# One ring for all loads, alternating K and V, and a column-tiled PV in a decode block with a 32768-row cache

## The chip, the cores and the metric

The kernel runs on one core of one Trainium2 chip; the other cores are idle. The metric is the device time of the execution in microseconds (us). Executions of one kernel agree within 1% here. Engine names are those of the profile: PE is TensorE (PEld its weight loads), DVE is VectorE, ACT is ScalarE, POOL is GpSimd, SP is SyncE, which in this kernel only issues the loads and the output.

## The reference, cut to what matters

A transformer block for one new token, batch 2, all in bf16. The cache is large, everything else is small:

```python
B, Sq, D = (2, 1, 1024);  Hq, Hkv, Sk, Dh = (32, 4, 32768, 128);  F = 3584
mod = silu(c) @ w_mod                       # [1024, 6144], gives sa, ca, ga, sb, cb, gb
h = layernorm(x) * (1 + ca) + sa
q = h @ wq                                  # 8 query heads for each of 4 KV heads
o = softmax(q k^T / sqrt(128)) v            # K and V: 2 x 4 x 32768 x 128 each
x = x + ga * (o @ wo)
h = layernorm(x) * (1 + cb) + sb
x = x + gb * (gelu(layernorm(h) @ w1 + b1) @ w2 + b2)   # the MLP has a layer norm of its own
```

K and V are 134.2 MB of the 178.3 MB that have to be read, each byte once. A (batch, KV head) pair is called a group below; there are 8, each with four chunks of K and four of V, 8192 rows or 2 MB to a chunk.

## The kernel before: the parts that matter

A small tracker writes the waits. It keeps, for every named region of memory, a token of its last writer and tokens of its readers since; an operation waits for the tokens of all regions that it names, and then leaves its own token on them.

```python
def _dep_tokens(self, E, reads, writes):
    ...                                    # last writer of each read region
    for w in self._expand(writes):         # last writer and readers of each written one
        reg = self._region(w)
        if reg[0] is not None:
            tokens.append(reg[0])
        tokens.extend(reg[1])
    ...
def _record(self, token, reads, writes):
    for w in writes:                       # the operation becomes last writer of ALL it names
        reg = self._region(w)
        reg[0] = token
        reg[1] = []
    ...
```

Loads go through six slots of 16 KB per partition, used in turn, plus fixed places for WO and W1. Each slot is one region, so two loads meet only when they use the same slot. SP issues the loads in the order of a list; a load waits until the slot's old content has been read.

```python
R = 6
slots = [at(f"slot{i}", [128, SLOT_BYTES // 2], BF16, slot_off(i)) for i in range(R)]
seq += kv("K", 0) + kv("K", 1) + kv("V", 0)            # four K chunks, four V chunks, ...
...
T.dma("sp", lambda e, dst=dst, src=src: e.dma_start(dst, src), key=key, writes=list(it.regions))
```

A whole group's K is transposed and multiplied (`QK(i)`), then the V of the group before (`PV(i-1)`). PV holds a 128 x 128 block of V stationary and streams 8 columns, 64 matmuls a chunk:

```python
T.inst("pe", lambda e, ...: e.matmul(psO[:, 0:HPG], lhsT=sl_view[:, t * 128:(t + 1) * 128],
                                     rhs=E_sb[j][:, :, tg], ...))
```

WO and W2 are loaded as `"(t p) n -> p t n"`, in rows of 2 KB. The layer norm inside the MLP is left out.

Of the kernel before, what the change touches and what calls it, by code (L numbers as in the profile page):

```python
# [12 lines left out]
HQ = 32  # L13
# [6 lines left out]
CH_ROWS = 8192  # L20
TPC = CH_ROWS // 128
NCH = S // CH_ROWS
# [6 lines left out]
R = 6  # L29
NKT = 8  # L30
PIPE = 3
NPKT = 4
NPS = 1
EVAC_PATTERN = ("dve", "act", "dve", "act", "dve", "dve", "act", "dve")
SLOT_BYTES = 16 * 1024
# [161 lines left out]
def bass_adaLN_cond__gqa_block_cached__mixer_channel_mlp__decode_kernel(  # L197
# [17 lines left out]
    ident = nc.alloc_sbuf_tensor("ident", [128, 128], BF16)  # L215
    identf = nc.alloc_sbuf_tensor("identf", [128, 128], FP32)
    onesf = nc.alloc_sbuf_tensor("onesf", [128, 128], FP32)
    x16 = nc.alloc_sbuf_tensor("x16", [16, 128], BF16)
    c16 = nc.alloc_sbuf_tensor("c16", [16, 128], BF16)
    b1m = nc.alloc_sbuf_tensor("b1m", [FT, 128], BF16)  # L220
    b2m = nc.alloc_sbuf_tensor("b2m", [KT8, 128], BF16)
    smallT = nc.alloc_sbuf_tensor("smallT", [128, 68], FP32)
    xT = smallT[:, 0:16].rearrange("p (b k) -> p b k", b=2)
    cT = smallT[:, 16:32].rearrange("p (b k) -> p b k", b=2)
    b1T = smallT[:, 32:60]
    b2T = smallT[:, 60:68]
    sgT = nc.alloc_sbuf_tensor("sgT", [128, 2, KT8], FP32)
    siluT = nc.alloc_sbuf_tensor("siluT", [128, 2, KT8], BF16)
    stat = nc.alloc_sbuf_tensor("stat", [128, 8], FP32)
    mean = nc.alloc_sbuf_tensor("mean", [128, 2], FP32)  # L230
    rstd = nc.alloc_sbuf_tensor("rstd", [128, 2], FP32)
    xc = nc.alloc_sbuf_tensor("xc", [128, 2, KT8], FP32)
    sq = nc.alloc_sbuf_tensor("sq", [128, 2, KT8], FP32)
    t1 = nc.alloc_sbuf_tensor("t1", [128, 2, KT8], FP32)
    hT = nc.alloc_sbuf_tensor("hT", [128, 2, KT8], BF16)
    modT = nc.alloc_sbuf_tensor("modT", [128, NMOD, 2], FP32)
    qacc = nc.alloc_sbuf_tensor("qacc", [128, 2 * HQ], FP32)
    qT = nc.alloc_sbuf_tensor("qT", [128, 2, HQ], BF16)
    attnT = nc.alloc_sbuf_tensor("attnT", [128, 2, HQ], BF16)
    yT = nc.alloc_sbuf_tensor("yT", [128, 2, KT8], FP32)  # L240
    x1T = nc.alloc_sbuf_tensor("x1T", [128, 2, KT8], FP32)
    h2T = nc.alloc_sbuf_tensor("h2T", [128, 2, KT8], BF16)
    zT = nc.alloc_sbuf_tensor("zT", [128, FT, 2], FP32)
    z2 = nc.alloc_sbuf_tensor("z2", [128, FT, 2], FP32)
    z3 = nc.alloc_sbuf_tensor("z3", [128, FT, 2], FP32)
    th = nc.alloc_sbuf_tensor("th", [128, FT, 2], FP32)
    gT = nc.alloc_sbuf_tensor("gT", [128, FT, 2], BF16)
    mT = nc.alloc_sbuf_tensor("mT", [128, KT8, 2], FP32)
    resT = nc.alloc_sbuf_tensor("resT", [128, 2, KT8], FP32)
    res_bf = nc.alloc_sbuf_tensor("res_bf", [128, 16], BF16)  # L250
    res16 = nc.alloc_sbuf_tensor("res16", [16, 128], BF16)
    m1 = [nc.alloc_sbuf_tensor(f"m1_{i}", [128, HPG], FP32) for i in range(2)]
    gm = [nc.alloc_sbuf_tensor(f"gm_{i}", [HPG, 1], FP32) for i in range(2)]
    diag = [nc.alloc_sbuf_tensor(f"diag_{i}", [HPG, HPG], FP32) for i in range(2)]
    negm = [nc.alloc_sbuf_tensor(f"negm_{i}", [128, HPG], FP32) for i in range(2)]
    rowsum = [nc.alloc_sbuf_tensor(f"rowsum_{i}", [128, HPG], FP32) for i in range(2)]
    rinv = [nc.alloc_sbuf_tensor(f"rinv_{i}", [128, HPG], FP32) for i in range(2)]

    KB = 1024
    ARENA = R * SLOT_BYTES + 32 * KB + 32 * KB + 32 * KB  # L260
    arena = nc.alloc_sbuf_tensor("arena", [128, ARENA], mybir.dt.uint8)
    abase = nc.lookup_mloc(arena).addr

    def at(name, shape, dtype, off):
        return nc.alloc_sbuf_tensor_at(name, list(shape), dtype, offset=abase + off)

    def slot_off(sl):
        return sl * SLOT_BYTES

    slots = [at(f"slot{i}", [128, SLOT_BYTES // 2], BF16, slot_off(i)) for i in range(R)]  # L270
    regA = R * SLOT_BYTES
    regB = regA + 32 * KB
    regC = regB + 32 * KB
    wo_blk = [at("wo0", [128, 16, DM], BF16, regA), at("wo1", [128, 16, DM], BF16, regB)]
    w1p = [at(f"w1p{k}", [128, F], BF16, (regA + k * 7 * KB) if k < 4 else (regB + (k - 4) * 7 * KB)) for k in range(6)]
    for i in range(2):
        for q in range(4):
            T.interval(f"wo{i}q{q}", (regA if i == 0 else regB) + q * 8 * KB, (regA if i == 0 else regB) + (q + 1) * 8 * KB)
    for k in range(6):
        off = (regA + k * 7 * KB) if k < 4 else (regB + (k - 4) * 7 * KB)  # L280
        T.interval(f"w1p{k}", off, off + 7 * KB)
    S_sb = at("S_sb", [128, HPG, NCH * TPC], FP32, regC)
    E_sb = [at(f"E_sb{i}", [128, HPG, NCH * TPC], BF16, regC + 8 * KB + i * 4 * KB) for i in range(2)]
    KT_sb = [at(f"KT_sb{i}", [128, 8, 128], BF16, regC + 16 * KB + i * 2 * KB) for i in range(NKT)]
    assert 16 + 2 * NKT <= 32

    psKT = [nc.alloc_psum_tensor(f"psKT{i}", [128, 1024], BF16) for i in range(NPKT)]
    psS = [nc.alloc_psum_tensor(f"psS{i}", [128, 512], FP32) for i in range(NPS)]
    psO = nc.alloc_psum_tensor("psO", [128, 512], FP32)
    psM = nc.alloc_psum_tensor("psM", [128, 512], FP32)  # L290
    psX = nc.alloc_psum_tensor("psX", [128, 512], FP32)

    T.inst("pool", lambda e: e.memset(ident[:, :], 0.0), writes=["ident"])
    T.inst("pool", lambda e: e.affine_select(out=ident[:, :], in_=ident[:, :], compare_op=ALU.not_equal, fill=1.0,
                                             base=0, pattern=[[-1, 128]], channel_multiplier=1), reads=["ident"], writes=["ident"])
    T.inst("pool", lambda e: e.memset(identf[:, :], 0.0), writes=["identf"])
    T.inst("pool", lambda e: e.affine_select(out=identf[:, :], in_=identf[:, :], compare_op=ALU.not_equal, fill=1.0,
                                             base=0, pattern=[[-1, 128]], channel_multiplier=1), reads=["identf"], writes=["identf"])
    T.inst("pool", lambda e: e.memset(onesf[:, :], 1.0), writes=["onesf"])

    T.dma("act", lambda e: e.dma_start(x16[:, :], A_x.rearrange("b o (k p) -> (b o k) p", p=128)), key="ld", writes=["x16"])
    T.dma("act", lambda e: e.dma_start(c16[:, :], c.rearrange("b (k p) -> (b k) p", p=128)), key="ld", writes=["c16"])
    T.dma("act", lambda e: e.dma_start(b1m[:, :], B_b1.rearrange("(f p) -> f p", p=128)), key="ld", writes=["b1m"])
    T.dma("act", lambda e: e.dma_start(b2m[:, :], B_b2.rearrange("(f p) -> f p", p=128)), key="ld", writes=["b2m"])

    class Item:
        def __init__(self, kind, i=0, cc=0, nslots=1, fixed=None):
            self.kind, self.i, self.cc, self.nslots, self.fixed = kind, i, cc, nslots, fixed
            self.pos = None
            self.view = None  # L310
            self.regions = None
            self.issued = False

    def kv(kind, i):
        return [Item(kind, i, cc) for cc in range(NCH)]

    def woq(i, qs):
        return [Item("WO", i, q, fixed="AB") for q in qs]
    K4 = kv("K", 4)
    V3 = kv("V", 3)  # L320
    seq = [Item("WMODH", 0, nslots=2)] + [Item("WQ", k) for k in range(KT8)]
    seq += kv("K", 0) + kv("K", 1) + kv("V", 0)
    seq += [Item("MODB", 0), Item("MODB", 1)] + kv("K", 2) + kv("V", 1)
    seq += [Item("MODB", 2), Item("MODB", 3)] + kv("K", 3) + kv("V", 2)
    seq += [Item("MODB", 4), Item("MODB", 5)] + woq(0, [0, 1]) + K4[0:2] + woq(0, [2, 3]) + K4[2:4]
    seq += [Item("MODB", 6), Item("MODB", 7)] + woq(1, [0, 1]) + V3[0:2] + woq(1, [2, 3]) + V3[2:4]
    seq += kv("K", 5) + kv("V", 4)
    seq += kv("K", 6) + kv("V", 5)
    seq += kv("K", 7) + kv("V", 6)
    seq += [Item("W1", k, fixed="AB") for k in range(4)] + kv("V", 7) + [Item("W1", k, fixed="AB") for k in range(4, 6)]  # L330
    seq += [Item("W1", k) for k in range(6, KT8)] + [Item("W2", j) for j in range(4)]
    lookup = {}
    rpos = 0
    for it in seq:
        lookup[(it.kind, it.i, it.cc)] = it
        if it.fixed is None:
            if it.nslots == 2 and (rpos % R) == R - 1:
                rpos += 1
            it.pos = rpos
            rpos += it.nslots  # L340
            sl = it.pos % R
# [11 lines left out]
            elif it.kind == "W2":  # L353
                it.view = at(f"w2v{it.i}", [128, 7, DM], BF16, slot_off(sl))
# [65 lines left out]
    def need(kind, i, cc=0):  # L420
        it = lookup[(kind, i, cc)]
        if not it.issued:
            issue_until(kind, i, cc)
# [314 lines left out]
```

## Time and profile before

Median 445.67 us of 3 runs (445.67 to 447.52) when the prediction was made.

| what | value | where it is read |
|---|---|---|
| bytes read | 178.28 MB | page, part 3 |
| share of the load queue | 96.7% of 16 engines' span | page, part 3 |
| PE busy | 309.0 of 445.5 us | page, part 1 |
| stream where nothing holds it | 420 to 433 GB/s | page, part 2 |

First the page of the kernel before, parts 1 to 3: busy time, the busy tenths and GB/s of the load engines in 40 slices of 11.1 us, and the queue that carries the loads (packets, MB, share).

```profile
PE 309.0 (69%) x7805; PEld 295.2 (66%) x7805; DVE 157.9 (35%) x294; ACT 143.3 (32%) x251; POOL 1.3 (0%) x9
...
DMA  8999999999999999999999999999999999999990
GB/s 316 421 425 433 419 423 431 420 344 424 425 430 420 427 427 419 414 413 410 417 413 403 428 425 430 422 384 415 430 424 418 427 382 383 427 425 414 394 369 34
...
q1 hardware_dynamic: 21616, 178.27, 96.7%
```

The load engines are busy in nearly every slice: the kernel is bound by the stream, and only the dips (344, 384, 382, 394, 369) and the two ends are to be had. (The 403 to 417 of slices 17 to 22, 178 to 245 us, fall where WO is loaded, in 2 KB rows.) What SP waited for before it could issue a load (SP's own waits; total us, times, longest us):

```profile
SPq L184 <- PE psKT L540: 194.6, 28, 18.0
SPq L184 <- PE psO L595: 77.3, 24, 9.8
...
SPq L184 <- PE psS L468: 13.3, 1, 13.3
```

Nearly every such wait is for PE: mostly the transposes (L540) or PV (L595) still read the slot. While earlier loads are queued, such a wait costs nothing. It costs where the queue runs dry; in stretches of ten microseconds (columns: busy us and number for PE, PEld, DVE, ACT and POOL, granted PE clock, share of the load engines, GB/s):

```profile
90.00:100.00 10.00, 9.39 (x283) 9.02 (x279) 5.15 (x7) 4.03 (x5) 0.00 (x0) 0.98 0.92 339
290.00:300.00 10.00, 8.98 (x228) 8.49 (x224) 5.40 (x9) 5.08 (x6) 0.00 (x0) 1.00 0.96 383
...
420.00:430.00 10.00, 4.95 (x153) 4.74 (x153) 2.57 (x15) 1.49 (x2) 0.00 (x0) 0.50 1.05 387
430.00:440.00 10.00, 6.74 (x247) 6.62 (x244) 2.33 (x12) 0.25 (x1) 0.00 (x0) 0.50 0.50 183
```

The first two are such dry spells. At 420 to 430 us the engines are fully busy (1.05) but move only 387 GB/s: this is W2, in 2 KB rows. At 430 to 440 us the stream ends, and compute alone follows.

### The profile page before, as it was taken

What the parts mean: (1) busy time and instruction counts of PE and PEld (TensorE: products, weight loads), DVE (VectorE), ACT (ScalarE), POOL (GpSimd) and SP (SyncE); (2) the same over time, 40 slices, a digit from 0 to 9 for tenths busy, and PEclk for the clock granted to TensorE, in tenths of its full rate; (3) what the DMA queues carried; (4) which work ended last, traced back from release to release, by engine and by line L of the source; (5) the groups of instructions that cost most, each with busy time, mean ns of one, the idle gap of its engine ahead of it and who ended that gap; (6) DMA issues with size and microseconds to landing.
All of it is one profiled execution on the core that took longest, in us unless ns stands there. A gap on an engine that the chain in (4) does not pass through costs nothing.

```text
span 445.5 us, 16705 instructions
## 1 busy us (share of the span) xinstructions
PE 309.0 (69%) x7805; PEld 295.2 (66%) x7805; DVE 157.9 (35%) x294; ACT 143.3 (32%) x251; POOL 1.3 (0%) x9
## 2 busy tenths in 40 slices
PE   1445987996986698638684258887977698755555
PEld 1445877895986598638574158886976588744455
DVE  1101656551652265215351004551643065400221
ACT  2001556630751166024250004640752065305100
POOL 1000000000000000000000000000000000000000
PEclk9999996995996599657696555995896579855555
DMA  8999999999999999999999999999999999999990
GB/s 316 421 425 433 419 423 431 420 344 424 425 430 420 427 427 419 414 413 410 417 413 403 428 425 430 422 384 415 430 424 418 427 382 383 427 425 414 394 369 34
DMA packets 21807, 179.35 MB, mean 403 GB/s; under 512 B 1770, under 2 KB 1770, under 8 KB 11498
## 3 DMA queue, kind: packets, MB, share of 16 engines
q1 hardware_dynamic: 21616, 178.27, 96.7%
q8 instruction: 61, 1.00, 0.9%
q14 instruction: 8, 0.07, 0.0%
q10 hardware_dynamic: 122, 0.02, 0.0%
HBM read 178.28 MB, written 0.00 MB: 400 GB/s over the span
## 4 chain that ended last, share of the span: by engine, by line
PE 52%; DMA 19%; issue 11%; ACT 9%; SPq 6%; DVE 3%; ACTq 0%; DVEq 0%
PE psKT L540 23%; PE psO L595 10%; DMA slot_53<-in_A_k_cache_dram 10%; PE psS L520 8%; SPq L396 5%; DMA wqv_77<-in_A_wq_dram 5%; DMA slot_54<-in_A_v_cache_dram 4%; PE psM L607 3%; ACT KT_sb_67 L550 3%; ACT S_sb L525 3%; ACT KT_sb_72 L550 2%; ACT E_sb_65 L576 1%; PE psM L572 1%; PE psM L478 1%; PE psM L567 1%
## 5 line engine op out<-in xcount | busy, mean ns | idle before, releaser
L550 ACT ACTIVATE KT_sb_72<-psKT 128x1024 bf16<-128x1024 bf16 x32 | 32.7, 1023 | 44.7 <-PE psKT L540 44.7
L550 ACT ACTIVATE KT_sb_67<-psKT 128x1024 bf16<-128x1024 bf16 x25 | 25.6, 1024 | 58.1 <-PE psKT L540 58.1
L576 ACT ACTIVATE E_sb_64<-S_sb,negm 128x256 bf16<-128x256 f32 x32 | 16.2, 506 | 78.1 <-DVE negm L574 77.3
L540 PE MATMUL psKT<-ident,slot_53 128*128 128x128 bf16 x384 | 35.5, 255 | 8.2 <-DMA slot_53<-in_A_k_cache_dram 8.2
L576 ACT ACTIVATE E_sb_65<-S_sb,negm 128x256 bf16<-128x256 f32 x32 | 16.2, 506 | 61.8 <-DVE negm L574 61.0
L553 DVE COPY KT_sb_70<-psKT 128x1024 bf16<-128x1024 bf16 x32 | 22.1, 692 | 36.2 <-PE psKT L540 36.2
L540 PEld LDWEIGHTS psKT<-ident,slot_53 128*128 128x128 bf16 x384 | 28.7, 116 | 8.4 <-DMA slot_53<-in_A_k_cache_dram 8.3
L540 PE MATMUL psKT<-ident,slot_51 128*128 128x128 bf16 x320 | 28.5, 251 | 4.7 <-DMA slot_51<-in_A_k_cache_dram 4.7
L540 PE MATMUL psKT<-ident,slot_54 128*128 128x128 bf16 x384 | 29.3, 218 | 1.2 <-issue 1.2
L598 DVE TENSOR_TENSOR attnT<-psO,rinv 128x8 bf16<-128x8 f32 x8 | 1.3, 167 | 79.2 <-PE psO L595 79.2
L553 DVE COPY KT_sb_66<-psKT 128x1024 bf16<-128x1024 bf16 x32 | 22.1, 692 | 19.6 <-PE psKT L540 19.4
L553 DVE COPY KT_sb_73<-psKT 128x1024 bf16<-128x1024 bf16 x32 | 22.1, 692 | 19.3 <-PE psKT L540 19.3
L553 DVE COPY KT_sb_68<-psKT 128x1024 bf16<-128x1024 bf16 x32 | 22.1, 692 | 17.9 <-PE psKT L540 17.9
L540 PE MATMUL psKT<-ident,slot_49 128*128 128x128 bf16 x320 | 27.0, 240 | 1.3 <-issue 1.3
L540 PEld LDWEIGHTS psKT<-ident,slot_51 128*128 128x128 bf16 x320 | 23.3, 114 | 5.4 <-DMA slot_51<-in_A_k_cache_dram 4.8
L550 ACT ACTIVATE KT_sb_69<-psKT 128x1024 bf16<-128x1024 bf16 x25 | 25.7, 1028 | 3.3 <-PE psKT L540 3.3
L540 PE MATMUL psKT<-ident,slot_50 128*128 128x128 bf16 x320 | 24.4, 218 | 0.3 <-issue 0.3
L540 PE MATMUL psKT<-ident,slot_52 128*128 128x128 bf16 x320 | 24.3, 218 | 0.0
L540 PEld LDWEIGHTS psKT<-ident,slot_49 128*128 128x128 bf16 x320 | 21.6, 108 | 1.4 <-issue 1.4
L553 DVE COPY KT_sb_71<-psKT 128x1024 bf16<-128x1024 bf16 x32 | 22.1, 691 | 1.0 <-PE psKT L540 0.8
L540 PEld LDWEIGHTS psKT<-ident,slot_54 128*128 128x128 bf16 x384 | 21.8, 97 | 0.0
L525 ACT ACTIVATE S_sb<-psS 128x512 f32<-128x512 f32 x32 | 19.0, 593 | 7.9 <-PE psS L520 7.9
(195 smaller groups left out, 517.1 us busy)
## 6 DMA issues: line engine op xcount, KB each, us to landing
slot_53<-in_A_k_cache_dram SPq DMA_DIRECT2D x6, 2048.0 KB, 15.6
slot_54<-in_A_k_cache_dram SPq DMA_DIRECT2D x6, 2048.0 KB, 17.6
slot_51<-in_A_v_cache_dram SPq DMA_DIRECT2D x6, 2048.0 KB, 17.1
slot_52<-in_A_v_cache_dram SPq DMA_DIRECT2D x6, 2048.0 KB, 19.8
slot_49<-in_A_k_cache_dram SPq DMA_DIRECT2D x5, 2048.0 KB, 17.1
slot_50<-in_A_k_cache_dram SPq DMA_DIRECT2D x5, 2048.0 KB, 20.3
slot_51<-in_A_k_cache_dram SPq DMA_DIRECT2D x5, 2048.0 KB, 19.2
slot_52<-in_A_k_cache_dram SPq DMA_DIRECT2D x5, 2048.0 KB, 19.2
```

The lines of the kernel that those rows point to most:

```text
L396: T.dma("sp", lambda e, dst=dst, src=src: e.dma_start(dst, src), key=key, writes=list(it.regions))
L478: T.inst("pe", lambda e, jc=jc: e.matmul(psM[:, 288 + jc * 2:290 + jc * 2], lhsT=wv[:, jc * 128:(jc + 1) * 128], rhs=siluT[:, :, kb], star ...
L520: T.inst("pe", lambda e, sbk=sbk, sp=sp, kn=kn, jj=jj: e.matmul(psS[sbk][:, sp * HPG:(sp + 1) * HPG], lhsT=KT_sb[kn][:, jj, :], rhs=qT[:, ...
L525: T.inst("act", lambda e, sbk=sbk, col0=col0: e.activation(S_sb[:, :, col0:col0 + 64], psS[sbk][:, 0:512].rearrange("p (t h) -> p h t", h= ...
L540: T.inst("pe", lambda e, kq=kq, jj=jj, sl_view=sl_view, t=t: e.transpose(psKT[kq][:, jj * 128:(jj + 1) * 128], sl_view[:, t * 128:(t + 1) ...
L550: T.inst("act", lambda e, kq=kq, kn=kn: e.activation(KT_sb[kn][:, :, :], psKT[kq][:, 0:1024].rearrange("p (a n) -> p a n", a=8), ACT.Copy) ...
L553: T.inst("dve", lambda e, kq=kq, kn=kn: e.tensor_copy(KT_sb[kn][:, :, :], psKT[kq][:, 0:1024].rearrange("p (a n) -> p a n", a=8)), reads=[ ...
L567: T.inst("pe", lambda e: e.matmul(psM[0:HPG, 0:128], lhsT=m1[j][:, :], rhs=identf[:, :], start=True, stop=True), reads=[f"m1_{j}", "identf ...
L572: T.inst("pe", lambda e: e.matmul(psM[:, 128:128 + HPG], lhsT=onesf[0:HPG, :], rhs=diag[j][:, :], start=True, stop=True), reads=["onesf", ...
L576: T.inst("act", lambda e, h=h: e.activation(E_sb[j][:, h, :], S_sb[:, h, :], ACT.Exp, bias=negm[j][:, h:h + 1], scale=SCALE, accum_out=row ...
L595: T.inst("pe", lambda e, t=t, sl_view=sl_view, tg=tg: e.matmul(psO[:, 0:HPG], lhsT=sl_view[:, t * 128:(t + 1) * 128], rhs=E_sb[j][:, :, tg ...
L607: T.inst("pe", lambda e, wv=wv, t=t, cch=cch: e.matmul(psM[:, col0 + cch:col0 + cch + 1], lhsT=wv[:, t % 16, cch * 128:(cch + 1) * 128], r ...
```

## The change

The intent: keep the stream full from the first byte to the last. All loads go in order through one ring of 160 KB per partition; a K chunk and the V chunk of five steps earlier are used in each step, so that memory comes free evenly; WO and W2 are read in long rows; PV takes a quarter of the matmuls; and the MLP's layer norm, which the reference has, is put in. The core of the diff, cut:

```diff
-R = 6
-SLOT_BYTES = 16 * 1024
+VLAG = 5
+RING = 160 * 1024
...
+    def add(key, shape, src):
+        nbytes = int(np.prod(shape)) * 2
+        off = 0
+        if stream:
+            off = stream[-1].off + stream[-1].nbytes
+            if off + nbytes > RING:
+                off = 0
...
+    for k in range(KT8):
+        add(("wmod", k), [6 * DM], ...)                # 12 KB
+    for k in range(4):
+        add(("wq", k), [2, HQ * D], ...)               # 16 KB
+    for n in range(NK + VLAG):
+        if n < NK: add(("K", n), [TPC, D], ...)        # 16 KB
+        if n - VLAG >= 0: add(("V", n - VLAG), ...)    # 16 KB; a WO quarter, 16 KB, after every eighth V
+    ...                                                # w1: four of 14 KB; w2: 16, 16, 16, 8 KB
+    def need(*key):
+        it = by_key[key]
+        while pos[0] <= it.n:
+            cur = stream[pos[0]]
+            old = [o.reg for o in stream[:cur.n] if o.off < cur.off + cur.nbytes and cur.off < o.off + o.nbytes]
+            T.dma("sp", ..., key=f"d_{cur.reg}", writes=[cur.reg] + old)
+            pos[0] += 1
...
-                e.matmul(psO[:, 0:HPG], lhsT=sl_view[:, t * 128:(t + 1) * 128], rhs=E_sb[j][:, :, tg], ...)
+                e.matmul(psO[32 * q:32 * q + 32, :], lhsT=E_sb[j][:, tg // 4, :, :] (32 columns: 8 heads x 4 rows),
+                         rhs=it.view[:, t4 * 4:t4 * 4 + 4, :] (512 columns), ...)     # q = t4 % 4
...
-  A_wo[r0:r0 + 512, :].rearrange("(t p) n -> p t n", p=128)
+  A_wo[g * 1024:(g + 1) * 1024, :].rearrange("(p j) n -> p j n", j=8)
...
+    layernorm(hmid[:, :, :], ["hmid"])
```

PV now makes four times the products it needs (each of 4 rows against each of 4 V blocks); after a group, a few DVE operations and one matmul pick the diagonal blocks.

## The prediction

> **What bounds the kernel now.** The memory stream. The page counts 178.28 MB read, DMA share 96.7%; in ten-microsecond stretches it moves 420 to 433 GB/s where nothing holds it; PE is busy 309.0 us of 445.5. The Trainium skill ("HBM Reference", Specifications (TRN2)) gives about 425 GB/s for a core that streams alone; this trace agrees. 178.28 MB at 424 GB/s is 420.5 us, so only some 25 us are to be had:
> - start: 306 GB/s in the first 10 us, 2.8 us lost;
> - stalls, where the slot to be refilled is still being read (SP waits for transposes and PV): 339 GB/s at 90-100 us, 383 at 290-300, 378 and 373 at 360-380; about 5.3 us;
> - loads in 2 KB rows (W2: 399 and 387 GB/s at 410-430; WO alike): about 3 us;
> - tail: the stream stops near 434.7 us (183 GB/s at 430-440); GELU, W2 and the output take the last 10.8 us.
>
> **What the change does.**
> 1. Ring: 160 KB of in-order stream against six 16 KB slots plus fixed regions; K and V of a step are used together, so a buffer is free soon after it lands. SP's waits become harmless: minus 5.2 us.
> 2. Rows of WO 16 KB, of W2 8 KB: minus 3 us. Fewer PE instructions to fetch (512 PV matmuls for 2048): minus 0.4.
> 3. Tail: after V's last chunk remain WO, W1, W2: 16.8 MB, 39.5 us of stream. The chain under it: last PV 2, picking the diagonal blocks 5, WO 2, then before's chain from WO to the end (418.4 to 445.5, 27 us) plus 4 for the second layer norm: about 40 us. So W2's last block (32 matmuls, 27 ns each) and before's 3.7 us from the last W2 matmul to the end follow the last byte: 5 us where 10.8 were. Minus 5.5. The second layer norm is hidden.
> 4. PV before: 128 matmuls in 3.57 us, with pauses of 2.6 ("issue"): 2.4 us a chunk. After: 16 matmuls of 512 columns; a transpose of 128 columns takes 60 ns at full clock, so 240 ns each: 3.8 us in series, 1 to 1.6 if the column tiles overlap. The skill ("TensorEngine Tiling (Array Packing)", Theoretical Speedup) allows up to 4x; no run here shows it yet. A K chunk takes PE 5.8 us (distance of score evictions). A K and V pair costs PE 7 to 7.5 us (9.7 in series) against 9.9 of stream (4.19 MB): off the path, barely so in series. ACT and DVE need about 5 us each per pair.
>
> **Sum.** 445.7 - 5.2 - 3.4 - 5.5 = 431; pure stream 420.5 + 2.8 + 5 + 2 for instruction fetch is 430. **Predicted 430 us, 8 in 10 between 424 and 439.** Faster by over 2% (below 436.8): 0.85; within 2%: 0.13; slower: 0.02.
>
> **What the profile would show.** Right: 415 GB/s or more in every slice from the second to the last but one; stream ending about 5 us before the span; PV 1 to 1.6 us a chunk; PE waiting for K or V loads; the last chain through W2's last load. Wrong: slices below 400 in the middle (ring or PE holds the stream); PE never waiting for K (tiles in series); W2 starting well after its last load (layer norms, or W1 with its weights strided by 4 columns, slower than 27 ns each).
>
> **What would make it wrong.** Column tiles in series at a lower PE clock: PE-bound, 440 or more. The exponentials (5.5 us of ACT in one lump) blocking evictions beyond the slack. A tail chain 5 us longer. A different stream rate with K and V alternating.

## The result, and the profile after

534.51 us median of 4 runs (533.38 to 537.57), against 446.43 of before in the same rounds. Ratios here are the mean time of one kernel's runs over that of the other's in the same rounds, so not quite the ratio of the medians; this one is 1.197 (95% interval 1.192 to 1.202). The change made the kernel a fifth slower where 3.5% faster had been forecast.

The page of the changed kernel, the same lines as above (slices of 13.3 us):

```profile
PE 312.0 (59%) x6035; PEld 275.5 (52%) x6035; DVE 164.1 (31%) x344; ACT 160.8 (30%) x266; POOL 1.3 (0%) x9
...
DMA  8999688987779786996889786997869958887665
GB/s 354 428 420 432 270 318 317 430 365 295 318 316 429 312 350 234 424 428 244 345 343 430 313 345 264 362 428 314 321 255 427 424 192 351 333 375 285 263 224 199
...
q1 hardware_dynamic: 14112, 178.27, 83.1%
```

PE's busy time hardly moved, but the stream has holes in the whole middle and tail, with full speed (424 to 432) in between. The engines are idle in the holes (tenths of 5 to 8), so it is not a slower stream but an interrupted one. The prediction had named slices under 400 in the middle as the sign that "ring or PE holds the stream". Which of them, SP's waits tell:

```profile
SPq L339 <- DMA V<-in_A_v_cache_dram: 201.2, 13, 30.2
SPq L339 <- DMA K<-in_A_k_cache_dram: 186.0, 14, 29.8
SPq L339 <- DMA w<-in_B_w_dram: 53.7, 5, 19.5
SPq L185 <- DMA w<-in_B_w_dram: 8.1, 1, 8.1
SPq L339 <- DMA wo<-in_A_wo_dram: 6.9, 1, 6.9
```

This is the line to notice. Before, SP waited for PE. Now it waits 13 + 14 + 5 + 1 + 1 = 34 times for a *load to land* before it issues another load. Loads of K and V write different places and need nothing of each other. The chain of waits in order of time (start us, us, what), one lap of the ring; its short PE and SP pieces are left out:

```profile
88.98 30.69 DMA V<-in_A_v_cache_dram
119.69 7.38 DMA K<-in_A_k_cache_dram
...
127.08 0.33 SPq L339
...
127.46 12.89 DMA K<-in_A_k_cache_dram
...
151.29 30.60 DMA V<-in_A_v_cache_dram
181.92 7.26 DMA wo<-in_A_wo_dram
189.19 0.33 SPq L339
...
189.57 12.10 DMA V<-in_A_v_cache_dram
```

From 119.69 to 127.08 us exactly one load is under way: it was issued when the one before it had landed (88.98 + 30.69), and the next was issued when it had landed itself. Alone it takes 7.38 us, where 2.097 MB at the 429 GB/s of a full slice would take 4.9. No other load is queued, ahead of it or behind it, at that moment.

And PE waits for K, not the other way round. The groups of the changed kernel (columns as in the page's part 5: busy us, mean ns; then the idle time before them and what ended it):

```profile
L541 PE MATMUL psKT<-ident,K 128*128 128x128 bf16 x2048 | 196.5, 254 | 103.7 <-DMA K<-in_A_k_cache_dram 103.7
...
L468 PE MATMUL psO<-V,E_sb 128*32 128x512 bf16 x512 | 40.8, 448 | 27.1 <-DMA V<-in_A_v_cache_dram 27.1
```

### Where the 34 waits come from

They can be derived from the source. `old` lists every item, of any age, whose bytes the new one overlaps. The load names them as `writes`, for a good reason: it has to wait for their readers. But the tracker then makes the load the *last writer of each of them*, dead items included. A dead item under two later ones ties these together. The eight 12 KB modulation items do just that, for good, because they stay in `stream`:

```
ring, KB   0        12   16     24      32  36          48
dead       | wmod0  | wmod1     | wmod2     | wmod3     |
live       | chunk A     | chunk B      | chunk C       |
```

Chunk A overlaps wmod1 and marks it. Chunk B overlaps wmod1 too, finds A's load as its last writer, and waits until A has *landed*. wmod2 ties C to B likewise. At 48 KB both grids meet again (3 x 16 = 4 x 12), so the next chunk is free, and the same pattern follows from 48 to 96 KB; above that lie 16 KB items only. That is four false waits in each lap of ten loads. In the tail the 14 KB items of W1 shift the grid, and each of the eight loads but two (W1's first and third) waits for its predecessor. Going through the 88 loads with these rules gives 34 waits for the load just before: 28 among K, V and WO and 6 among W1 and W2. The profile counted the same: 13 + 14 + 1 and 5 + 1.

### The profile page after: what moved, and what is told of

The parts are those of the page before. It is cut to its first block, busy times and chain, and to the rows that moved or that the text cites. A ratio compares the mean times of both kernels' runs of the same rounds, so it can differ in the third digit from the quotient of the medians.

```text
span 531.6 us, 13037 instructions
## 1 busy us (share of the span) xinstructions
PE 312.0 (59%) x6035; PEld 275.5 (52%) x6035; DVE 164.1 (31%) x344; ACT 160.8 (30%) x266; POOL 1.3 (0%) x9
## 4 chain that ended last, share of the span: by engine, by line
DMA 86%; PE 7%; SPq 6%; issue 1%; DVE 0%
DMA K<-in_A_k_cache_dram 37%; DMA V<-in_A_v_cache_dram 35%; DMA w<-in_B_w_dram 13%; SPq L339 6%; PE psKT L541 5%; DMA wo<-in_A_wo_dram 1%; PE psS L436 1%; DVE KT_sb L547 0%; PE psM L489 0%; PE psM L478 0%; PE psS L586 0%; PE psO L468 0%; PE psM L454 0%; PE psM L448 0%; PE psM L592 0%
## 5 line engine op out<-in xcount | busy, mean ns | idle before, releaser
L541 PE MATMUL psKT<-ident,K 128*128 128x128 bf16 x2048 | 196.5, 254 | 103.7 <-DMA K<-in_A_k_cache_dram 103.7
L541 PEld LDWEIGHTS psKT<-ident,K 128*128 128x128 bf16 x2048 | 150.9, 115 | 119.8 <-DMA K<-in_A_k_cache_dram 116.6
L545 ACT ACTIVATE KT_sb<-psKT 128x1024 bf16<-128x1024 bf16 x96 | 98.3, 1024 | 260.0 <-PE psKT L541 250.4
L547 DVE COPY KT_sb<-psKT 128x1024 bf16<-128x1024 bf16 x160 | 109.1, 690 | 210.6 <-PE psKT L541 209.7
L436 PE MATMUL psS<-qT,KT_sb 128*128 128x8 bf16 x2048 | 93.1, 169 | 4.5 <-ACT KT_sb L545 4.5
L436 PEld LDWEIGHTS psS<-qT,KT_sb 128*128 128x128 bf16 x2048 | 88.0, 103 | 5.5 <-ACT KT_sb L545 4.7
L468 PE MATMUL psO<-V,E_sb 128*32 128x512 bf16 x512 | 40.8, 448 | 27.1 <-DMA V<-in_A_v_cache_dram 27.1
L457 ACT ACTIVATE E_sb<-S_sb,negm 128x256 bf16<-128x256 f32 x64 | 32.5, 508 | 7.5 <-DVE negm L455 5.6
L442 DVE TENSOR_REDUCE m1c<-S_sb 128x8 f32<-128x512 f32 x32 | 22.0, 688 | 14.3 <-ACT S_sb L441 12.7
L457 ACT ACTIVATION_READ_ACCUMULATOR E_sb<-S_sb,negm 128x1 f32 x64 | 12.0, 187 | 0.0
```

What stands on the lines that cost most here:

```text
L436: pe(lambda e, t=t, jj=jj: e.matmul(ps[:, t * HPG:(t + 1) * HPG], lhsT=KT_sb[kn][:, jj, :], rhs=qT[:, b, g * HPG:(g + 1) * HPG], start=Tru ...
L442: dve(lambda e: e.tensor_reduce(m1c[:, :, cc], Sc, AX.X, ALU.max), reads=[f"S_sb{i % 2}_{cc}"], writes=[f"m1c{cc}"])
L457: act(lambda e, h=h: e.activation(E_sb[j][:, :, h, :], S_sb[j][:, h, :].rearrange("p (u t) -> p u t", t=4), ACT.Exp, bias=negm[j][:, h:h + ...
L468: pe(lambda e, t4=t4, tg=tg, q=q: e.matmul(psO[32 * q:32 * q + 32, :], lhsT=E_sb[j][:, tg // 4, :, :].rearrange("p h t -> p (h t)"), rhs=i ...
L541: pe(lambda e, kq=kq, jj=jj, w=it.view, t=t: e.transpose(psKT[kq][:, jj * 128:(jj + 1) * 128], w[:, t, :], ident[:, :]), reads=[it.reg, "i ...
L545: act(lambda e, kn=kn, src=src: e.activation(KT_sb[kn][:, :, :], src, ACT.Copy), reads=[f"psKT{kq}"], writes=[f"KT_sb{kn}"])
```

## The experiments

The theory: these 34 waits, and nothing else, turned a gain into a loss; each drains the queue and costs about 3 us ((534.5 - 431) / 34). Rival A: PE, the evictions or the column tiles hold the ring. Rival B: alternating K and V, or the long rows, stream more slowly.

Two words on correctness. All runs passed the comparison with the reference, also those that compute something wrong. The attention output is a mean over 32768 small random values, so it hardly shows in the result: here a pass says little about PV or WO. The false waits are a matter of time only.

### 1. The waits taken away, in two independent ways

**e1_no_relink.** A load still waits for everything that the old items' bytes require, but leaves its token on its own region only:

```diff
-    def dma(self, E, fn, key, reads=(), writes=()):
+    def dma(self, E, fn, key, reads=(), writes=(), after=()):
...
-        waits = self._compute_waits(E, self._dep_tokens(E, reads, writes))
+        waits = self._compute_waits(E, self._dep_tokens(E, reads, list(writes) + list(after)))
...
-    T.dma("sp", ..., writes=[cur.reg] + old)
+    T.dma("sp", ..., writes=[cur.reg], after=old)
```

> Edit: a load still waits for everything that earlier occupants of its bytes need, but no longer becomes the 'last writer' of those dead occupants, so no load waits for the load just ahead of it. Main theory (34 of the 88 loads wait for the landing of the load just before them, each costing some 3 us of stream): 430 us, range 424 to 436, no SP wait for a load's landing except at the output, stream above 415 GB/s in all middle slices. Rival A (PE or the evictions hold the ring, column tiles too slow): stays above 500 us. Rival B (alternating K and V, or the larger rows, give a slower stream): above 480 us with DMA share near 1 and GB/s below 400.

Measured: 431.49 us (431.33 to 431.69), before 446.88 in the same rounds, ratio 0.966 (0.963 to 0.968). The page's GB/s, and SP's largest waits:

```profile
GB/s 328 434 421 426 436 426 426 430 426 429 429 429 429 427 433 426 431 429 424 429 430 427 430 429 429 429 429 430 426 430 431 425 430 430 423 431 424 427 387 116
```

```profile
SPq L339 <- PE psS L436: 185.3, 31, 11.3
SPq L339 <- PE psM L505: 45.5, 3, 15.5
SPq L339 <- PE psO L468: 32.2, 24, 7.9
...
SPq L185 <- DMA K<-in_A_k_cache_dram: 15.4, 10, 3.1
```

The stream is full from the second slice to the last but two. SP waits a lot, and harmlessly: nine loads are queued ahead of it. One expectation was too strict: ten short waits for a landing remain. Each load waits, first for the landing and then for the readers of what it replaces, and with the ring full that old load is sometimes still on its way; these are true waits, and the stream never feels them.

**e2_aligned.** The waits are left alone; the places are changed, so that no dead item lies under two live ones:

```diff
-            off = stream[-1].off + stream[-1].nbytes
+            off = -(-(stream[-1].off + stream[-1].nbytes) // 16384) * 16384
```

> Edit: waits left as the change has them; every item is put at a multiple of 16 KB in the ring, so that no dead item lies under two later ones. Main theory: no link is left, within 1.5% of the run without re-marking, about 430 us (the 12 KB items now take 16 KB of ring, which delays two early loads at most). If removing the re-marking had helped in another way than through these links, this one stays near 534 us.

Measured: 431.39 us (431.26 to 431.48), ratio 0.965. The same time by another route, and SP's list of waits names no landing of a load any more. Rivals A and B fall: everything they blame is still in both kernels.

### 2. Fewer and more of them

**e3_wmod_aligned** aligns only the modulation items. By the same rules the 28 waits among K, V and WO go. The tail, whose loads now begin at another place of the ring, has 7 waits where the change has 6. (The expectation below puts the change's 34 at 27 and 7; it is right about the 7 of this run.)

```diff
-            off = stream[-1].off + stream[-1].nbytes
+            off = stream[-1].off + (16384 if stream[-1].key[0] == 'wmod' else stream[-1].nbytes)
```

> Edit: only the eight modulation items are put at multiples of 16 KB; W1's 14 KB items keep 7 links in the tail, the 27 links among K, V and WO are gone. Main theory, linear in links (104 us over 34 links, 3.1 us each): 430 + 7 x 3.1 = 452 us, range 445 to 460. If the K and V links cost nothing and the tail does all: stays near 534. If the tail's links are hidden: 430.

Measured: 451.96 us (451.13 to 453.00). SP's waits count the seven (2 + 5), and the last six slices carry the loss:

```profile
SPq L185 <- DMA w<-in_B_w_dram: 48.2, 2, 41.5
...
SPq L339 <- DMA w<-in_B_w_dram: 36.5, 5, 8.4
```

```profile
GB/s 333 430 424 426 431 431 429 421 431 426 428 431 429 426 434 425 430 428 431 425 432 426 431 429 425 432 426 426 434 428 429 429 426 429 282 203 294 232 276 147
```

**e4_all_links** starts from e1 and makes every load from the thirteenth on wait, by design, for the landing of the one before: 76 waits.

```diff
+    T.dma("sp", ..., writes=[cur.reg], after=old,
+          landed=[stream[cur.n - 1].reg] if cur.n >= 12 else [])   # waits for that load's token only
```

> Edit: without the re-marking, but each load from the thirteenth on waits by design for the landing of the load before it: 76 links for 34. Main theory: a 2 MB load alone takes 7.3 us from issue to landing (profile of the change) against 4.9 in the stream, so 50 us of first loads + about 68 x 7.3 + 8 smaller ones x 6.3 + 5 is about 600 us, range 580 to 665 (3.1 us per link would give 666). Rivals that blame PE or the K and V order: near 534.

Measured: 638.12 us (636.68 to 639.12). From part 6 of its page (count, KB each, median us from issue to landing), a load alone:

```profile
K<-in_A_k_cache_dram SPq DMA_DIRECT2D x32, 2048.0 KB, 7.4
V<-in_A_v_cache_dram SPq DMA_DIRECT2D x32, 2048.0 KB, 7.4
```

| kernel | waits for the load just before | us | more than e1 | for each wait |
|---|---|---|---|---|
| e1_no_relink | 0 | 431.5 | | |
| e3_wmod_aligned | 7 | 452.0 | 20.5 | 2.9 |
| the change | 34 | 534.5 | 103.0 | 3.0 |
| e4_all_links | 76 | 638.1 | 206.6 | 2.7 |

The last column is "more than e1" divided by the number of waits. Over a tenfold range of doses each wait costs 2.7 to 3.0 us. The larger part of it is 7.4 - 4.9 = 2.5 us, what a lone load takes beyond its share of a full stream.

**e9_two_back** asks why such a wait costs. It is e4 with `stream[cur.n - 2]`, so that one load is always still in flight behind the awaited one.

> Edit: as in the run with all links, but each load from the thirteenth on waits for the landing of the load TWO before it. If a link costs because the pipe runs empty (about 2.4 us between one load's landing and full flow of the next), one load left in flight (4.9 us of stream) covers it: 431 to 440 us. If it were the waiting on landings as such that costs: near 638 us as with one back.

Measured: 434.68 us (433.20 to 435.95). SP waits for landings as often as before, and it costs 3 us in all:

```profile
SPq L339 <- DMA V<-in_A_v_cache_dram: 149.1, 32, 5.3
SPq L339 <- DMA K<-in_A_k_cache_dram: 144.4, 32, 5.0
```

So waiting for a landing is not what costs. What costs is the empty queue: with one 2 MB load (4.9 us of stream) in flight, the start of the next is almost covered. Not wholly: from 40 to 360 us this stream moved 421 GB/s where e1 moved 429, some 6 us; part of that comes back at the end, where the sixteenths of a load land closer together than in e1 (section 4).

### 3. The other parts of the prediction, tried on the mended kernel

**e6_no_ln2**: the MLP's layer norm taken out of e1, `modulate` writing the MLP's input directly.

> Edit, on the version without re-marking: the second layer norm taken out (its result then differs a little). Prediction's step 3 says that it hides under the loads of W1 and W2: 431.5 within 0.3%. If the tail's chain were what ends last: about 4 us less, 427.5.

Measured: 431.58 us (431.52 to 431.72). The added layer norm costs nothing; it hides under the loads of W1 and W2. Because this run equals e1 and shares its chip with the next two, it is their yardstick.

**e7_rows_2k**: WO as `"(j p) n -> p j n"`, W2 as `"(q j p) n -> p q j n"`: 2 KB rows, result wrong.

> Edit, on the version without re-marking: WO and W2 loaded in 2 KB rows again (rows permuted, so the result is wrong on purpose), 15.7 MB in all. Prediction's step 2 puts the rows at 3 us: 434.5. If row length doesn't matter at this size: 431.5 within 0.3%, and the 399 and 387 GB/s of before had another cause.

Measured: 433.78 us (433.61 to 433.98), 2.2 more. From 400 to 410 us the stream moves 387 GB/s, where e1 moves 427 (e1 first, then e7; columns as in the stretches above). Expected were 3 us.

```profile
400.00:410.00 10.00, 7.39 (x202) 7.25 (x203) 1.00 (x7) 1.49 (x2) 0.00 (x0) 0.50 1.02 427
```

```profile
400.00:410.00 10.00, 6.66 (x180) 6.49 (x180) 1.61 (x10) 1.49 (x2) 0.00 (x0) 0.50 0.98 387
```

**e5_old_pv**: PV with V stationary, 64 matmuls a chunk (and `psO` cleared once at the start), result wrong.

```diff
-            e.matmul(psO[32 * q:32 * q + 32, :], lhsT=E_sb[j][:, tg // 4, :, :]..., rhs=it.view[:, t4 * 4:t4 * 4 + 4, :]..., ...)
+            for tt in range(4):
+                e.matmul(psO[:, 0:HPG], lhsT=it.view[:, t4 * 4 + tt, :], rhs=E_sb[j][:, tg // 4, :, tt], ...)
```

> Edit, on the version without re-marking (431.5 us): PV in the old form, 64 matmuls a chunk with V stationary and 8 moving columns, in place of 16 in four column tiles (the result is wrong on purpose). In the profile without re-marking PE waits 55 us in all for K, so there is slack: PV costs about 1.8 to 2.4 us a chunk for 1.05, PE some 8.5 us a pair of chunks against 9.8 of stream. If PV is off the path: 431.5 within 1% (up to 435). If the column tiles were what bought the time: 440 or more.

Measured: 434.12 us (433.95 to 434.17), 2.5 more than e6. Within the stated 1%, but clear of noise, and the expectation gave no reason for it. Section 4 returns to it.

**e8_one_tile**: e1 with `q = 0` for every PV matmul, so that all use one column tile (and `psO` cleared once at the start); result wrong.

> Edit, on the version without re-marking: all 16 PV matmuls of a chunk go to the first column tile in place of four tiles in turn (the result is wrong on purpose). If the tiles run side by side: the 16 matmuls take about 3.5 to 3.9 us at full clock for 1.05; PE then needs some 10 us a pair with the exponentials' stalls, against 9.8 of stream, so 435 to 450 us with PE on the path. If they don't run side by side anyway: 431.5 and 1.05 us again.

Measured: 432.49 us (432.36 to 432.58), against 431.33 (431.24 to 431.79) of **e12_repeat**, e1 again in the same set:

> The version without re-marking again, unchanged, as the yardstick of this set: 431.5 us within 0.3.

One chunk's PV at full clock in the order of time (start us, us), first e1, then e8:

```profile
216.56 1.05 PE L468 MATMUL psO<-V,E_sb 128*32 128x512 bf16 x16
```

```profile
208.44 3.63 PE L469 MATMUL psO<-V,E_sb 128*32 128x512 bf16 x16
```

The tiles do run side by side, 3.5 times as fast as one (the Trainium skill, "TensorEngine Tiling (Array Packing)", Theoretical Speedup, allows up to 4x). The expected 435 us or more did not come: with the matmuls in series PE still keeps up, but only just. From 100 to 360 us it is busy 246.2 of 260 us (201.5 in e12), and the clock granted to it there was 0.97 of full speed, against 0.84 in e12. What the run would have taken at e12's clock is not shown. PE's waits for K shrink, e1 first, then e8:

```profile
PE psKT L541 <- DMA K<-in_A_k_cache_dram: 54.7, 19, 6.1
```

```profile
L542 PE MATMUL psKT<-ident,K 128*128 128x128 bf16 x2048 | 163.0, 225 | 10.9 <-DMA K<-in_A_k_cache_dram 10.9
```

### 4. What is left in the last microseconds

Each load raises its semaphore in 16 steps, and the trace has the times of these steps. They are taken here, as an inference, for the landings of sixteen shares of the load, one on each of the 16 load engines that the page counts. How far the first and the last of the 16 are apart, for the last load of each kernel (worked out from the trace's landing records; the trace does not say which engine made which step):

| kernel | spread of the last load's 16 steps, us | time, us |
|---|---|---|
| the change | 0.4 | 534.5 |
| e9_two_back | 2.3 | 434.7 |
| e12_repeat (e1) | 9.0 | 431.3 |
| e11_more_code | 10.4 | 433.2 |
| e5_old_pv | 11.6 | 434.1 |

In e12 the spread is 1.6 us at 27 us, 4.8 at 203 and 8.7 at 362: it grows in jumps of 1.0 to 1.4 us that hit one share at a time. In the end eight of the sixteen steps come within 2.8 us of the first, and the other eight 7.2 to 9.0 us after it. The program waits for all 16, so the slowest counts. The page books the fetching of instructions on the same engines, in packets of 16 KB that each take about 0.94 us, 47 of them in e1 and 59 in e5_old_pv. The guess: fetched code delays the shares that have to carry it.

The traces bear the guess out. Add up how far the 16 steps of a load lie behind its first. In e12 this sum grows by 1.6 us for each packet of code fetched by then (correlation 0.999 over its loads), to 73.5 us at the last load. In e5_old_pv it ends at 90.1 us: 16.6 more for 12 packets more, 1.4 us each.

**e11_more_code** puts 2048 tiny memsets on the idle POOL of e1 and changes nothing else:

```diff
+    for _ in range(2048):
+        T.inst("pool", lambda e: e.memset(scrap[0:1, 0:1], 0.0), writes=["scrap"])
```

> Edit, on the version without re-marking: 2048 tiny memsets more on the idle GpSimd, nothing else; no engine on the path does more, but at least 8 more packets of 16 KB of instructions are fetched. Old PV form: 12 packets more (59 for 47) and 2.6 us more, 0.2 us a packet, while in the trace eight of the sixteen shares of each load fall ever further behind the other eight. If instruction fetch delays those eight: plus 1.4 to 2 us, 433 to 433.5, spread of the last loads' landings above 10 us. If old PV's 2.6 us came from PE: 431.5.

Measured: 433.17 us (432.88 to 433.64), 1.8 more than e12. The queues (packets, MB, share), first of e12, then of e11:

```profile
q8 instruction: 47, 0.77, 0.6%
...
q14 instruction: 7, 0.06, 0.0%
```

```profile
q8 instruction: 47, 0.77, 0.6%
...
q14 instruction: 23, 0.19, 0.1%
```

The time came as expected, the details only in part. POOL's code came in 16 more packets on another queue, of 8 KB each (0.13 MB), and the eight late shares stayed where they were (7.3 to 8.8 us behind the first). Instead a ninth joined them and became the last of all, at 10.4 us: seven steps are early here, where e12 has eight. The sum of the lags is 8.6 us larger than in e12, 0.5 us for each packet of 8 KB. So more fetched code, with no more work on any engine of the path, does lengthen this stream-bound kernel. That e5's 2.5 us has the same cause fits well (12 packets more, a spread 2.6 us wider) but is not isolated: e5 also gives PE more to do. That the memsets' own writes disturb nothing was not tested. Since the jumps were seen only as steps of semaphores, the assignment to engines stays an inference.

**e10_split_last** splits W2's last 1 MB load in two, so that half of its matmuls run before the last byte lands.

> Edit, on the version without re-marking: W2's last 1 MB load in two of 512 KB, so that half of its 32 matmuls run before the last byte lands. The tail after the last landing is 1.0 us of matmuls + 2.4: minus 0.4 us, 431.1. If the added load costs more than it hides: 431.5 or above.

Measured: 430.94 us (430.79 to 431.00) against 431.33 (431.24 to 431.79) of e12 in the same set: the runs do not overlap, a gain of 0.4 us as expected. Its ratio to before is 0.963 (0.960 to 0.965). It is the fastest version found and beats both kernels.

## Why the prediction was wrong, point by point

1. **The step that failed is step 1**: "K and V of a step are used together, so a buffer is free soon after it lands. SP's waits become harmless: minus 5.2 us." The first half was right, the second did not follow. It looked at when a buffer *is* free and not at what the program *waits for* before it calls it free. The line `writes=[cur.reg] + old` was read as "waits for old readers"; it also re-marks dead regions, and 34 of 88 loads waited for the load just ahead. In place of minus 5.2 us, the runs showed plus 103 (534.5 against 431.5 without the re-marking). This could have been found blind, for it follows from the source and the item sizes alone.
2. **Rows (step 2).** Forecast 3 us, measured 2.2 (e7 against e6). Right mechanism, a little too large.
3. **Code to fetch (step 2).** Forecast 0.4 us, which fits a count of bytes (12 packets of 16 KB at 424 GB/s are 0.46 us). PV's old form costs 2.5 us (e5 against e6), probably through fetching; by bytes the term was several times too small.
4. **Tail (step 3).** That the second layer norm is hidden is shown (e6). The tail after the last landing was put at 5 us; in e12 the last load lands at 425.9 us of 429.9, so 4.0. In the kernel before, the last load lands at 436.9 of 445.5, so its tail was 8.6 and not 10.8 us (the prediction had taken the end of the stream from its rate), and the step brought 4.6 us where 5.5 were forecast. In the unmended kernel this step could not hold, because W1 and W2 came one at a time.
5. **PV and PE (step 4).** A chunk's PV was put at 1 to 1.6 us, and takes 1.05. "Off the path, barely so in series" is shown, at the higher clock that e8 was granted: in series it costs 3.63 us a chunk and 1.2 us of the whole.
6. **The sum.** 430 us was forecast for the change as it was meant. Without the false waits it takes 431.5. If the parts simply add, the 15.4 us between before and e1 in the same rounds (446.88 - 431.49) split into rows 2.2 (forecast 3), PV's form 2.5 (0.4), tail 4.6 (5.5) and a rest of 6.1 for the stalls (5.2). The rest was not measured by itself. That the sum came so close is in part luck: errors of both signs cancelled.
7. **What would make it wrong** named four dangers: PE, exponentials, the tail's chain, the stream's rate. None of them came true. The waits that the program itself writes were not on the list. The signs had been chosen well enough, though: slices below 400 in the middle pointed at the ring.

## What to carry to other kernels

When buffers of different sizes share a ring, a dependency tracker must forget what has been overwritten: wait for the old regions, but leave your mark only on your own, or keep all items on one grid. When a stream-bound kernel has holes, look first at what the issuing queue waited for: waits for PE behind a full queue cost nothing, but a load that waits for the load just before it costs the start-up of a transfer each time (2.7 to 3.0 us here), while waiting for the one before that is nearly free. And in a change meant to remove waits, count the waits that remain, from the source, before predicting.

## What the Trainium skill lacked or had wrong

- "DMA: Bandwidth & Descriptors", Rules for kernel authors, gives 128 partitions and at least 1 MiB per transfer for maximum bandwidth. For transfers issued one at a time that was not enough here: those of 2 MB took 7.4 us each (e4), 2.097 MB / 7.4 us = 283 GB/s, against 429 with several queued. One more in flight brought back all but 3 us of 207 (e9). The page does state a fixed cost of about 2.0 us per transfer (Anatomy of one DMA, for the path through GpSimd); the 2.5 us seen here on loads issued by SP agree roughly.
- "DMA: Bandwidth & Descriptors", Specifications, puts the minimum for line rate at 512 B. Rows of 2 KB moved 387 GB/s with the engines fully busy (before, 420 to 430 us, share 1.05), where e1's rows of 7 to 16 KB moved 422 to 434 (ten-microsecond stretches from 10 to 410 us); 15.7 MB in 2 KB rows cost 2.2 us (e7).
- "Runtime: NRT & Kernel Launch", Instruction fetch mechanics, calls the cost of crossing a 16 KiB boundary mostly hidden. In a kernel bound by its loads it is not: 0.13 MB more of code on an idle engine cost 1.8 us (e11). No page tells that the sixteen shares of a load drift apart with each packet of code, to 9.0 us by the end of e12.
- "HBM Reference", Specifications (TRN2), gives about 425 GB/s to a core that streams alone. e1's slices, from the second to the last but two, show 421 to 436: confirmed, if a little low.
